# Weight conversion moved from GpSimd to the vector engine, and a part of q's rotation the other way

## The chip, the cores and the metric

One Trainium2 chip, one of its cores. The time is that of one execution on the device, in microseconds (us). The engines are named as the profile names them: PE (matrix multiplies) with PEld (its loads of stationary operands), DVE (vector engine), ACT (scalar engine), POOL (GpSimd), SP (the queue that issues the DMAs).

## What is computed

Rotary attention followed by two feed-forward layers, all in float32 from inputs of which the weights are float64:

```python
q, k, v: (4, 8, 576, 64)
rotate(x) = concat([x1 * cos - x2 * sin, x1 * sin + x2 * cos])      # x1, x2: halves of the last axis
attn = softmax(rotate(q) @ rotate(k).T / 8)                          # per batch and head
x  = (attn @ v) as (2304, 512)
h  = x @ w_in                                                        # (512, 2048)
g  = where(h >= 1, h, where(h <= -1, 0, (h + 1) ** 2 / 4));  x = g @ w_out
h2 = x @ w_in2;  g2 = s * relu(h2) ** 2 + b;                 out = g2 @ w_out2
```

## The kernel before

The heads are taken two at a time: 16 pairs, each with 9 units of queries. For a unit PE makes the scores `sc` (two buffers in PSUM), DVE takes their maximum (`nm`, line 342), ACT the exponential (`p`, line 347), PE turns `p` over and multiplies by v. Every product is made with split operands: a high part of few bits and a low part, so that three products of high and low stand for one of full precision.

A feed-forward layer has 16 slices of weights, each converted in two halves of 128 x 512 (64 conversions in all: 32 per layer). Half of the first layer's slices work beside the attention ("fill" work: `h` and `y` products of the tokens whose attention is done); from about 450 us on only the feed-forward layers are left, and PE runs through `hps` and `yps`.

**Conversion of half a slice** (`convert`, lines 115 to 134). A weight arrives as 8 bytes (`wraw`, two buffers, loaded by SP). ACT scales the upper four bytes into `wa` (line 127). DVE shifts them (128), sets the sign (129) into `wm`, keeps the exponent alone in `wa` (130), and multiplies it by 16 lower bits of the weight (131). ACT rounds `wm` to the high part `hi` (132). POOL takes `wm - hi` and adds `wa`: the low part `lo`. Each of these two POOL operations is cut in two pieces of 256 columns (`pool_tt`, line 91), so one conversion issues 4 POOL instructions. `wa` and `wm` have one buffer each: the next conversion's line 127 waits until POOL has read `wa` of this one. The result goes to the slice's tile `w`, or for 8 halves of the attention's time back into `wraw`, to be parked in DRAM.

**Rotation of the next pair** (`rope_pair`, lines 273 to 283). For each pair `i + 1` while pair `i` runs: POOL multiplies q by the table (line 279, 4 pieces of 288), DVE adds the two products (line 281), ACT writes the high part `qs` (294) and DVE the low part (295). The same for k is all POOL's, and ACT's for its high part (306).

Each engine works its instructions off in order. The order of the instructions in the attention's time is set by a planner from estimated times, with some instructions held behind others (`issue_after`); from line 708 on PE's order is the written one. `do_load` (line 530 on) places the conversions and the rotations: one conversion each two to six units, the rotation of q at unit 0 of each pair.

Of the kernel before, what the change touches and what calls it, by code (L numbers as in the profile page):

```python
# [11 lines left out]
U32 = mybir.dt.uint32  # L12
U16 = mybir.dt.uint16
AF = mybir.ActivationFunctionType
ALU = mybir.AluOpType
# [48 lines left out]
def kernel(ctx, tc, qq, kk, vv, tab, ww1, ww2, s, b, out):  # L64
    nc = tc.nc
# [14 lines left out]
    def pool_tt(out, in0, in1, op, dim=-1):  # L80

        n = out.shape[dim]
        free = 1
        for x in out.shape[1:]:
            free *= x
        k = min(n, -(-free // PW))
        for i in range(k):
            c = [slice(None)] * len(out.shape)
            c[dim] = slice(n * i // k, n * (i + 1) // k)
            c = tuple(c)  # L90
            nc.gpsimd.tensor_tensor(out=out[c], in0=in0[c], in1=in1[c], op=op)  # L91
# [3 lines left out]
    def split(dst_hi, dst_lo, src, hi_eng, lo_eng):  # L95
        if hi_eng is nc.scalar:
            made.append(nc.scalar.copy(dst_hi, src).ins)  # L97
        else:
            hi_eng.tensor_copy(dst_hi, src)
        tt = pool_tt if lo_eng is nc.gpsimd else nc.vector.tensor_tensor  # L100
        tt(out=dst_lo, in0=src, in1=dst_hi, op=ALU.subtract)  # L101
# [7 lines left out]
    class Slice:  # L109
# [5 lines left out]
        def convert(self, raw, pools, hi, lo):  # L115
            if not wide:
                split(hi, lo, raw, nc.scalar, nc.gpsimd)
                return


            top = raw.bitcast(F32).rearrange("p (n t) -> p n t", t=2)[:, :, 1]
            low = raw.bitcast(U16).rearrange("p (n t) -> p n t", t=4)[:, :, 1]
            pool = pools[self.f * 2 + self.made & 1 if len(pools) > 1 else 0]
            a = pool.tile([P, HW], F32, tag="wa", name="wa", bufs=WB)
            m = pool.tile([P, HW], F32, tag="wm", name="wm", bufs=WB)
            au, mu = a.bitcast(U32), m.bitcast(U32)
            nc.scalar.activation(a, top, AF.Copy, scale=2.0 ** -112)
            nc.vector.tensor_scalar(out=mu, in0=au, scalar1=3, scalar2=None, op0=ALU.logical_shift_left)
            nc.vector.scalar_tensor_tensor(out=mu, in0=au, scalar=0x80000000, in1=mu, op0=ALU.bitwise_and, op1=ALU.bitwise_or)  # L129
            nc.vector.tensor_scalar(out=au, in0=mu, scalar1=0xFF800000, scalar2=None, op0=ALU.bitwise_and)  # L130
            nc.vector.scalar_tensor_tensor(out=a, in0=low, scalar=2.0 ** -36, in1=a, op0=ALU.mult, op1=ALU.mult)
            nc.scalar.copy(hi, m)  # L132
            pool_tt(out=m, in0=m, in1=hi, op=ALU.subtract)
            pool_tt(out=lo, in0=m, in1=a, op=ALU.add)

        def load(self, stage, k):
            raw = stage.tile([P, HW], self.ww.dtype, tag="wraw", name="wraw", bufs=RB)
# [107 lines left out]
    def load_qk(i, nm, pieces=WHOLE):  # L245
        bb, hp = divmod(i, NP)
        t = att2.tile([P, 2, S], F32, tag="qkin", name=f"{nm}in", bufs=QB)
        for c in pieces:
            nc.sync.dma_start(out=t[:, :, c], in_=(qq if nm == "q" else kk)[bb, hp, :, :, c])
        qk_in[nm, i] = t  # L250

    def load_v(i):
        bb, hp = divmod(i, NP)
        t = att2.tile([P, 5, 2, D], F32, tag="vin", name="vin", bufs=VB)
        for out, src in ((t[:, :, 1], vv[bb, hp, :, :, 1]), (t[:D, :4, 0], vv[bb, hp, D:, :4, 0]), (t[D:, :4, 0], vv[bb, hp, :D, 1:, 0]), (t[D:, 4, 0], vv[bb, hp, :D, 0, 0])):
            nc.sync.dma_start(out=out, in_=src)
        v_in[i] = t
# [15 lines left out]
    def rope_pair(i, nm, mul, add, lo_eng, pieces=WHOLE):  # L273

        t = qk_in.pop((nm, i))
        tt = {nc.gpsimd: pool_tt, nc.vector: nc.vector.tensor_tensor}
        last = None
        for c in pieces:
            tt[mul](out=t[:, :, c], in0=t[:, :, c], in1=tab_sb[:, :, c], op=ALU.mult)
            r = t[:, 1, c]  # L280
            tt[add](out=r, in0=t[:, 0, c], in1=r, op=ALU.add)
            last = (lay_q if nm == "q" else lay_k)(i, t, c, lo_eng)
        return last
# [3 lines left out]
    def lay_q(i, t, c, lo_eng, heads=range(2)):  # L287

        st = stacks["q", i] = qs_t[i % 2]
        r = t[:, 1, c]  # L290
        for j in heads:
            own, other = SELF[j], SELF[1 - j]
            at = slice(j * QW + c.start, j * QW + c.stop)
            h = nc.scalar.activation(st[own, at], r[own], AF.Copy, scale=0.125)
            m = nc.vector.scalar_tensor_tensor(out=st[other, at], in0=r[own], scalar=0.125, in1=st[own, at], op0=ALU.mult, op1=ALU.subtract)  # L295
        return h.ins, m.ins
# [180 lines left out]
    def turned_by(t, c):  # L477
        nc.vector.tensor_tensor(out=t[:, :, c], in0=t[:, :, c], in1=tab_sb[:, :, c], op=ALU.mult)
        nc.vector.tensor_tensor(out=t[:, 1, c], in0=t[:, 0, c], in1=t[:, 1, c], op=ALU.add)
# [7 lines left out]
    hi, rest = lay_q(0, tq, QP[0], None, [0])  # L487
    with tc.issue_after(hi):
        first = lay_k(0, tk, HALVES[1], [nc.gpsimd, nc.gpsimd], [1])
    hi, rest = lay_q(0, tq, QP[0], None, [1])  # L490
# [39 lines left out]
    def do_load(n):  # L530
        if n < 2:
            with tc.issue_after(maxs[0] if n else rest):
                turned_by(tq, QP[n + 1])
                lay_q(0, tq, QP[n + 1], None)
        if n < len(units):
            i, k = units[n]
            if i + 1 < NPAIR:
                if k == (i == 0):
                    with ExitStack() if i else tc.issue_after(maxs[1]):
                        rope_pair(i + 1, "q", nc.gpsimd if i else nc.vector, nc.vector, None)  # L540
                elif k == 2:
                    with ExitStack() if i else tc.issue_after(exps[2]):
                        rope_pair(i + 1, "k", nc.gpsimd, nc.gpsimd, [nc.gpsimd, nc.vector])
                elif k == 3:
                    load_v(i + 1)
                elif k in (4, 6) and i + 2 < NPAIR:
                    load_qk(i + 2, "q" if k == 4 else "k")

        if n in range(33, 51, 2) or n in range(70, 110, 4):
            with tc.issue_after(exps[n - 14]):  # L550
                convert()

        if n in PARK_AT and parking:
            with tc.issue_after(exps[n - 4]):
                parking.pop(0).park(wst, scratch)
# [31 lines left out]
    def do_fill(n):  # L587
        if n < 48:
            return
        with tc.issue_after(exps[min(n, len(units)) - 4]):  # L590
            run_fill(0.62 if n < 76 else 0.92)

    acts = {"q": do_qk, "l": do_load, "t": do_t, "a": do_av, "f": do_fill}
    for n in range(len(units) + LA):
        with ExitStack() as st:
# [24 lines left out]
    def stage(src, chunks, dst, parts, slices, act, ahead, per):  # L620
# [33 lines left out]
        for i in range(len(steps) + GL):  # L654
# [39 lines left out]
            if i < len(steps):  # L694
                owed += per
                while owed >= 1:
                    with tc.issue_after(mark):
                        convert()
                    owed -= 1

    def cut(n0, n1, n):

        k = -(-(n1 - n0) // n)
        at = [n0 + (n1 - n0) // 16 * i // k * 16 for i in range(k + 1)]
        return [(a, b - a) for a, b in zip(at, at[1:])]
# [5 lines left out]
    a, b, c, d = cut(last, NT, N2A), cut(0, last, N2), cut(last, NT, N2), cut(0, NT, N2)  # L711
# [57 lines left out]
```

## Time and profile before

| | before |
|---|---|
| median of 3 runs | 1138.54 us (1137.49 to 1143.67) |
| profiled execution | 1140.24 us, span 1138.4 us |
| busy: PE, DVE, ACT, POOL | 1091.7, 600.3, 696.9, 536.2 us |
| mean granted PE clock | 0.995 |

The span runs from the first instruction's start to the last one's end. A busy time says how long an engine had an instruction, not whether it worked at its peak. "Idle before" names what ended an engine's wait.

### The profile page before, as it was taken

What the parts mean: (1) busy time and instruction counts of PE and PEld (TensorE: products, weight loads), DVE (VectorE), ACT (ScalarE), POOL (GpSimd) and SP (SyncE); (2) the same over time, 40 slices, a digit from 0 to 9 for tenths busy, and PEclk for the clock granted to TensorE, in tenths of its full rate; (3) what the DMA queues carried; (4) which work ended last, traced back from release to release, by engine and by line L of the source; (5) the groups of instructions that cost most, each with busy time, mean ns of one, the idle gap of its engine ahead of it and who ended that gap; (6) DMA issues with size and microseconds to landing.
All of it is one profiled execution on the core that took longest, in us unless ns stands there. A gap on an engine that the chain in (4) does not pass through costs nothing.

```text
span 1138.4 us, 18638 instructions
## 1 busy us (share of the span) xinstructions
PE 1091.7 (96%) x6720; PEld 981.3 (86%) x6720; DVE 600.3 (53%) x1003; ACT 696.9 (61%) x1472; POOL 536.2 (47%) x716
## 2 busy tenths in 40 slices
PE   3999999889999999999999999999999999999998
PEld 3666677778898989999999999998888889888887
DVE  6889898887676753454656555343333242221121
ACT  4777777766776775565555444476766756555543
POOL 7979887885572322355656624343443452011000
PEclk9999899999999999999999999999999999999999
DMA  7565755544564433455344434313322331220210
GB/s 223 166 183 168 190 149 177 175 134 155 165 180 148 134 110 89 157 161 166 109 145 139 147 100 120 100 55 104 105 70 90 104 110 54 90 81 29 67 51 34
DMA packets 89756, 140.46 MB, mean 123 GB/s; under 512 B 28864, under 2 KB 66752, under 8 KB 89664
## 3 DMA queue, kind: packets, MB, share of 16 engines
q1 hardware_dynamic: 89664, 139.27, 40.2%
q8 instruction: 53, 0.87, 0.3%
q14 instruction: 39, 0.32, 0.1%
HBM read 95.22 MB, written 30.74 MB: 111 GB/s over the span
## 4 chain that ended last, share of the span: by engine, by line
PE 78%; DVE 7%; DMA 4%; ACT 4%; POOL 4%; issue 2%; SPq 1%; POOLq 0%; ACTq 0%; DVEq 0%
PE hps L171 30%; PE yps L682 10%; PE yps L684 10%; PE yps L683 10%; PE sc L340 5%; PE h L171 3%; PE av L388 3%; PE tp L362 3%; PE y L171 2%; POOL kin L91 2%; DVE nm L342 2%; ACT p L347 2%; DMA kin<-in_k 1%; DVE qs L295 1%; DVE wm L129 1%
## 5 line engine op out<-in xcount | busy, mean ns | idle before, releaser
L171 PE MATMUL hps<-xh,w 128*128 128x464 f32 (+5 forms) x1216 | 344.5, 348 | 0.0
L171 PEld LDWEIGHTS hps<-xh,w 128*128 128x128 f32 x1216 | 221.8, 188 | 14.8
L682 PE MATMUL yps<-gh,w 128*128 128x464 f32 (+5 forms) x608 | 211.7, 348 | 0.5 <-ACT ys L465 0.5
L684 PE MATMUL yps<-gh,w 128*128 128x464 f32 (+5 forms) x608 | 211.6, 348 | 0.0
L171 PE MATMUL hps<-xl,w 128*128 128x464 f32 (+5 forms) x608 | 211.5, 348 | 0.0
L683 PE MATMUL yps<-gl,w 128*128 128x464 f32 (+5 forms) x608 | 211.4, 348 | 0.0
L91 POOL TENSOR_TENSOR xl<-xs,xh 128x232 fp32r<-128x232 f32 (+5 forms) x172 | 125.5, 758 | 171.2 <-ACT xh L97 170.9
L91 POOL TENSOR_TENSOR wm<-wm,w 128x256 f32<-128x256 f32 x112 | 100.3, 916 | 208.0 <-ACT w L132 167.1
L101 DVE TENSOR_TENSOR gl<-ar,gh 128x464 fp32r<-128x464 f32 (+1 forms) x80 | 59.0, 737 | 263.5 <-ACT gh L97 263.5
L340 PE MATMUL sc<-kh,qs 128*128 128x288 f32 x336 | 103.7, 330 | 32.6 <-ACT p L347 20.6
L342 DVE TENSOR_REDUCE nm<-sc 128x1 f32<-128x576 f32 x144 | 107.7, 752 | 39.7 <-PE sc L340 38.9
L347 ACT ACTIVATE p<-sc,nm 128x576 f32<-128x576 f32 x144 | 106.7, 743 | 32.6 <-DVE nm L342 32.0
L682 PEld LDWEIGHTS yps<-gh,w 128*128 128x128 f32 x608 | 114.1, 188 | 8.1 <-ACT ys L465 0.8
L683 PEld LDWEIGHTS yps<-gl,w 128*128 128x128 f32 x608 | 114.1, 188 | 7.5
L684 PEld LDWEIGHTS yps<-gh,w 128*128 128x128 f32 x608 | 114.1, 188 | 7.4
L171 PEld LDWEIGHTS hps<-xl,w 128*128 128x128 f32 x608 | 114.1, 188 | 7.3
L202 ACT ACTIVATE ar<-hps 128x464 f32<-128x464 f32 (+1 forms) x80 | 44.4, 555 | 121.7 <-PE hps L171 121.2
L340 PEld LDWEIGHTS sc<-kh,qs 128*128 128x128 f32 x336 | 65.1, 196 | 50.7 <-ACT p L347 28.8
L362 PE MATMUL tp<-ident,p 128*128 128x128 f32 x576 | 90.3, 281 | 5.5 <-ACT p L347 3.3
L340 PE MATMUL sc<-kz,qs 128*128 128x288 f32 x336 | 95.2, 303 | 0.0
L101 DVE TENSOR_TENSOR gl<-ac,gh 128x288 fp32r<-128x288 f32 (+3 forms) x112 | 72.6, 650 | 40.6 <-ACT gh L97 40.0
L91 POOL TENSOR_TENSOR w<-wm,wa 128x256 fp32r<-128x256 f32 x112 | 87.9, 803 | 0.2
(87 smaller groups left out, 1981.9 us busy)
## 6 DMA issues: line engine op xcount, KB each, us to landing
wraw<-in_ww SPq DMA_DIRECT2D x64, 512.0 KB, 3.8
kin<-in_k SPq DMA_DIRECT2D x15, 576.0 KB, 4.9
qin<-in_q SPq DMA_DIRECT2D x15, 576.0 KB, 3.9
kh<-kin SPq DMA_DIRECT2D x60, 144.0 KB, 2.6
xs<-y1d SPq DMA_DIRECT2D x32, 232.0 KB, 2.5
xs<-xd SPq DMA_DIRECT2D x44, 144.0 KB, 2.4
yd<-ys SPq DMA_DIRECT2D x40, 144.0 KB, 2.6
xd<-u SPq DMA_DIRECT2D x16, 288.0 KB, 2.4
```

The lines of the kernel that those rows point to most:

```text
L91: nc.gpsimd.tensor_tensor(out=out[c], in0=in0[c], in1=in1[c], op=op)
L101: tt(out=dst_lo, in0=src, in1=dst_hi, op=ALU.subtract)
L171: m = nc.tensor.matmul(out_ps, l, r, start=(i == 0), stop=(i == n - 1))
L202: nc.scalar.activation(r, h, AF.Relu)
L340: nc.tensor.matmul(sc[:, half, o:o + n], l, r[:, k0:k0 + n], start=m == 0, stop=m == len(todo) - 1)
L342: maxs[i * 9 + k] = nc.vector.tensor_reduce(out=nm, in_=sc[:, :, :288], axis=AX.XY, op=ALU.max, negate=True).ins
L347: exps[i * 9 + k] = nc.scalar.activation(p, sc[:, :, :288], AF.Exp, bias=nm, scale=1.0, accum_out=sums_t[i][:, col:col + 1]).ins
L362: m = nc.tensor.transpose(v[:, c, :], p[:, c * P:(c + 1) * P], ident)
L388: nc.tensor.matmul(ps[j * D:(j + 1) * D, :n], v[:, kt, j, :], pt[g][:, kt, j, :], start=kt == 0, stop=False)
L682: nc.tensor.matmul(acc, wh, gh, start=f == 0, stop=False)
L683: nc.tensor.matmul(acc, wh, gl, start=False, stop=False)
L684: nc.tensor.matmul(acc, wl, gh, start=False, stop=last)
```

## The change

Two edits. In `convert` the shifted bits are masked at once, so that `wm` is the high part before ACT copies it; the bits below the mask are taken from `wraw` as whole numbers, joined with the 16 lower ones, and scaled by the exponent into the low part. DVE now makes six instructions for a conversion instead of four, POOL none instead of four. The fifth of the six overwrites `wm`, which ACT's copy reads. In `do_load` the addition of q's two products for pairs 4 to 11 goes from DVE to POOL, where it is cut into two pieces of 288 columns.

```diff
-            nc.vector.tensor_scalar(out=mu, in0=au, scalar1=3, scalar2=None, op0=ALU.logical_shift_left)
+            nc.vector.tensor_scalar(out=mu, in0=au, scalar1=3, scalar2=0x7FFFF000, op0=ALU.logical_shift_left, op1=ALU.bitwise_and)
             nc.vector.scalar_tensor_tensor(out=mu, in0=au, scalar=0x80000000, in1=mu, op0=ALU.bitwise_and, op1=ALU.bitwise_or)
-            nc.vector.tensor_scalar(out=au, in0=mu, scalar1=0xFF800000, scalar2=None, op0=ALU.bitwise_and)
-            nc.vector.scalar_tensor_tensor(out=a, in0=low, scalar=2.0 ** -36, in1=a, op0=ALU.mult, op1=ALU.mult)
+            nc.vector.tensor_scalar(out=au, in0=raw.bitcast(U32).rearrange("p (n t) -> p n t", t=2)[:, :, 1], scalar1=0x1FF, scalar2=None, op0=ALU.bitwise_and)
+            nc.vector.scalar_tensor_tensor(out=a, in0=au, scalar=65536.0, in1=low, op0=ALU.mult, op1=ALU.add)
             nc.scalar.copy(hi, m)
-            pool_tt(out=m, in0=m, in1=hi, op=ALU.subtract)
-            pool_tt(out=lo, in0=m, in1=a, op=ALU.add)
+            nc.vector.tensor_scalar(out=mu, in0=mu, scalar1=0xFF800000, scalar2=None, op0=ALU.bitwise_and)
+            nc.vector.scalar_tensor_tensor(out=lo, in0=a, scalar=2.0 ** -36, in1=m, op0=ALU.mult, op1=ALU.mult)
...
-                        rope_pair(i + 1, "q", nc.gpsimd if i else nc.vector, nc.vector, None)
+                        rope_pair(i + 1, "q", nc.gpsimd if i else nc.vector, nc.gpsimd if 3 <= i < 11 else nc.vector, None)
```

## Rows read from the trace of the kernel before

**Rows 1.** Windows by stage: length, busy time (instructions), granted clock, DMA share, GB/s.

```profile
core 0: us, PE busy (x) PEld busy (x) DVE busy (x) ACT busy (x) POOL busy (x), PEclk, DMA share, GB/s
50.00:300.00 250.00, 228.79 (x1692) 185.84 (x1691) 207.22 (x343) 177.88 (x425) 194.00 (x251) 0.98 0.57 168
300.00:450.00 150.00, 147.57 (x1160) 132.31 (x1155) 91.28 (x173) 100.65 (x257) 54.42 (x80) 1.00 0.43 132
450.00:950.00 500.00, 499.47 (x2809) 474.25 (x2808) 228.75 (x377) 295.93 (x575) 229.70 (x303) 1.00 0.37 117
```

**Rows 2.** Windows for line 127 alone: it runs once for each conversion.

```profile
50.00:300.00 250.00, 12.28 (x18) 0.98 0.57 168
300.00:450.00 150.00, 4.03 (x6) 1.00 0.43 132
450.00:950.00 500.00, 26.84 (x40) 1.00 0.37 117
```

**Rows 3.** PE's timeline: start, length, instruction, [PE idle before it, releaser].

```profile
129.63 0.40 PE L340 MATMUL sc<-kh,qs 128*128 128x288 f32 x1 [1.84 <-ACT p L347]
...
189.11 0.40 PE L340 MATMUL sc<-kh,qs 128*128 128x288 f32 x1 [2.48 <-ACT p L347]
...
218.92 0.40 PE L340 MATMUL sc<-kh,qs 128*128 128x288 f32 x1 [2.97 <-ACT p L347]
...
242.34 0.40 PE L340 MATMUL sc<-kh,qs 128*128 128x288 f32 x1 [1.48 <-ACT p L347]
```

**Rows 4.** Chain of waits before the PE stall at 189 us: start, length, what.

```profile
183.81 0.70 POOL w L91
...
184.54 0.68 ACT wa L127
...
186.34 0.85 DVE wm L129
```

**Rows 5.** DVE's timeline around the PE stalls at 130 and 219 us.

```profile
126.45 1.27 DVE L281 TENSOR_TENSOR qin<-qin 128x576 f32<-128x576 f32 x1 [1.31 <-POOL qin L91]
...
215.67 0.62 DVE L128 TENSOR_SCALAR wm<-wa 128x512 uint32<-128x512 uint32 x1 [1.65 <-ACT wa L127]
```

**Rows 6.** Windows behind two of these stalls: PE's granted clock.

```profile
130.00:138.00 8.00, 7.23 (x37) 5.74 (x37) 5.53 (x9) 6.00 (x14) 6.84 (x11) 0.57 0.40 92
...
218.00:224.00 6.00, 5.08 (x26) 4.11 (x28) 5.20 (x9) 5.31 (x13) 4.89 (x6) 0.72 0.61 163
```

**Rows 7.** Lines by form, DVE, 50 to 300 us: count, busy us, mean ns, idle before.

```profile
L131 DVE SCALAR_TENSOR_TENSOR wa<-wraw,wa 128x512 f32<-128x512 uint16 x18 | 16.5, 916 | 0.3
L129 DVE SCALAR_TENSOR_TENSOR wm<-wa,wm 128x512 uint32<-128x512 uint32 x18 | 16.3, 904 | 0.3
...
L281 DVE TENSOR_TENSOR qin<-qin 128x576 f32<-128x576 f32 x11 | 12.5, 1134 | 6.6 <-POOL qin L91 6.6
L128 DVE TENSOR_SCALAR wm<-wa 128x512 uint32<-128x512 uint32 x18 | 11.0, 612 | 3.9 <-ACT wa L127 3.6
L130 DVE TENSOR_SCALAR wa<-wm 128x512 uint32<-128x512 uint32 x18 | 10.5, 584 | 0.2
```

**Rows 8.** Lines by form, POOL, 50 to 300 us.

```profile
L91 POOL TENSOR_TENSOR wm<-wm,w 128x256 f32<-128x256 f32 x32 | 28.2, 901 | 7.5 <-DVE wa L130 4.4 <-ACT w L132 2.0 <-ACT r L421 1.2
L91 POOL TENSOR_TENSOR w<-wm,wa 128x256 fp32r<-128x256 f32 x32 | 25.7, 818 | 0.2
L91 POOL TENSOR_TENSOR kin<-kin 128x288 f32<-128x288 f32 x21 | 18.8, 903 | 0.2
...
L91 POOL TENSOR_TENSOR wraw<-wm,wa 128x256 fp32r<-128x256 f32 x4 | 3.2, 792 | 0.0
L91 POOL TENSOR_TENSOR wm<-wm,wraw 128x256 f32<-128x256 f32 x4 | 3.1, 789 | 1.9 <-ACT wraw L132 1.9
```

**Rows 9.** Tile `wa`: count, ns of one (min/median/max), first and last start.

```profile
L129 DVE SCALAR_TENSOR_TENSOR wm<-wa,wm x64: 655/693/1304, 62.1 to 939.0; 128x512 uint32<-128x512 uint32 x64
L130 DVE TENSOR_SCALAR wa<-wm x64: 396/427/1027, 64.7 to 939.8; 128x512 uint32<-128x512 uint32 x64
L131 DVE SCALAR_TENSOR_TENSOR wa<-wraw,wa x64: 676/693/1282, 67.7 to 940.2; 128x512 f32<-128x512 uint16 x64
```

## The prediction

> **What bounds the kernel now.** First the windows by stage [rows 1]. From 450 us to 950 us PE has an instruction for 499.47 of 500 us: nothing done to DVE or POOL can shorten that, only lengthen it. From 300 to 450 us PE lacks 2.4 us. From 50 to 300 us it lacks 250 - 228.79 = 21.2 us, and there DVE is busy for 207.22 us (83%) and POOL for 194.00 us (78%). The first 50 us come before the first conversion, and the stretch behind 950 us after the last. So what the change can win is in these 21.2 us and in the time PE ran at a lower clock there. PE's timeline shows the four largest stalls of that stage [rows 3]: 1.84, 2.48, 2.97 and 1.48 us, 8.8 us together, each ended by an exponential of ACT. The other 12.4 us are many small ones. The chain of waits behind the stall at 189 us [rows 4] reads backwards from it: ACT's copy of a conversion's high part stood in front of the exponential; that copy waited for DVE's line 129, this for ACT's line 127, and line 127 started at the moment when POOL had finished with the single buffer `wa` of the conversion before. At 219 us DVE itself stood idle for 1.65 us for that line 127 [rows 5] with the maximum of the scores queued behind. At 130 us DVE waited 1.31 us for POOL's product of q and then took 1.27 us for the sum [rows 5], and the maximum behind it came late. The fourth, at 242 us, I count like the second without going further into it. Then the clock: in the 8 us behind the first stall PE was granted 0.57 and in the 6 us around the third 0.72 [rows 6], where full is 2.4 GHz and the lower level 1.2 GHz: 8 x 0.43 + 6 x 0.28 = 5.1 us of full-speed work lost, behind idle PE both times. What the edits can touch is therefore 8.8 + 5.1 = 13.9 us.
>
> **POOL, removed and added.** 18 of the 64 conversions lie in 50 to 300 us, 6 in 300 to 450, 40 behind [rows 2]. In the first stage POOL loses 28.2 + 25.7 + 3.2 + 3.1 = 60.2 us [rows 8]. It gains the sums of q for 8 pairs, two pieces each; the same form with the same shape is k's sum at 903 ns [rows 8]: 16 x 0.903 = 14.4 us. POOL goes from 194.0 to 148.2 us (59%), a quarter less.
>
> **DVE, added and removed.** The mask put into line 128 is a second operation of an instruction that runs anyway; I take its 612 ns [rows 7] as unchanged, since line 129 of the same width also makes two operations and what sets it apart is its second tensor. The mask of the exponent moves from fourth to fifth place at the same price. The multiplication of line 131 becomes a multiplication and an addition on two tensors, as before 916 ns. New are the low bits from `wraw` and the last product. The last product is line 131's or 129's form: 916 ns in this stage, 676 ns when nothing disturbs it [rows 7, 9]. For the low bits no row shows a one-tensor mask whose source steps over every other word: the dense one takes 584 ns in this stage and 396 ns at least [rows 7, 9], and line 131, which also reads `wraw` in steps, 916 ns. I take 584, the row of the same operation; less than 396 is excluded because no 512-column instruction of these lines is shorter. So 18 x (0.584 + 0.916) = 27.0 us are added, between 19.3 and 33.0. Pairs 4 to 11 lose line 281: 8 x 1.134 = 9.1 us [rows 7].
>
> VectorE: DVE Perf Modes of the Trainium skill (section What auto-detection actually checks) says that an instruction with a single source goes at two elements per cycle if source and destination lie in SBUF with fitting outer dimensions, and names no condition on the step for that mode. No run here shows it for a stepped source; by the page the stepped mask would cost what the dense one does, which leaves the sum as it is, and by the row of line 131 it would cost 18 x 0.332 = 6.0 us of DVE more.
>
> DVE's instructions also get longer when POOL is busy: in this stage lines 129, 130 and 131 average 904, 584 and 916 ns against medians of 693, 427 and 693 [rows 7, 9], 18 x (0.211 + 0.157 + 0.223) = 10.6 us. A quarter less POOL gives back a quarter, 2.5 us (bounds: 0 and, for all of it, 10.6). Net DVE gets 27.0 - 9.1 - 2.5 = 15.4 us more: 222.6 us, 89%. With the ends of the two new instructions it is 7.7 to 21.4 us.
>
> **What of this reaches PE.** (a) Stalls that go. At 130 us the wait and the sum in front of the maximum go (2.58 us against a stall of 1.84): all of it. At 219 us DVE's idle 1.65 us goes; the two long instructions of the conversion that follow remain. At 189 us, and so at 242, POOL's hold on `wa` goes but the conversion's own DVE and ACT work stays: half, 1.98 us. That is 5.5 of 8.8 us; the same share of the clock's 5.1 us is 3.2. Together -8.7 us, between 0 (something else is late just then) and -13.9.
> (b) The busier DVE. The 12.4 us of small stalls are the price of a DVE at 83%. If what waits in front of an engine grows as busy time over idle time, 207.2/42.8 = 4.84 becomes 222.6/27.4 = 8.12, and the small stalls grow by 0.68 x 12.4 = 8.4 us. Two score buffers cover part: I take half, +4.2 us, between 0 and, with the upper DVE load (10.7 for 8.12) and the full price, +15.0. Less than 0 is excluded by a load that is larger at both ends.
> (c) The new wait. The fifth instruction overwrites `wm` and must wait for ACT's copy; behind it on DVE stand the next maximum and the copies out of PSUM, for which ACT's exponential and PE wait. Between the two instructions the low bits and their sum take 0.58 + 0.92 = 1.5 us, while the copy itself starts when line 129 is done; so the wait shows only where ACT has much in front. The nearest row is DVE's wait for ACT at the start of a conversion, 3.6 us over 18 [rows 7]; a good quarter at PE, +1.0 us, between 0 and 3.6.
> (d) q's sum on POOL ends later: 2 x 0.903 = 1.81 us against 1.13, 0.67 us more for 8 pairs. ACT's split of q waits for it, with exponentials behind. It belongs to the next pair, so a whole pair of 9 units hides it: 0, and 5.4 us if ACT reaches it at once each time.
> (e) Later stages: between 300 and 450 us 6 conversions with DVE at 91 of 150 us: 0. From 450 to 950 us 40 x 1.5 = 60 us come to DVE's 228.75 of 500 [rows 1, 2]. PE hides them, working three steps behind the splits that DVE makes: 0. If that cover went, PE would wait for each conversion's last instruction, up to 40 x 0.92 us; nothing in PE's 499.47 us speaks for it.
>
> Sum: -8.7 + 4.2 + 1.0 = -3.5 us. Against the profiled execution's 1140.24 us (span 1138.4 and 1.84 around it) that is 1136.7; it lies 1.7 us above the median of the three runs, from which the forecast is 1138.54 - 3.5 = **1135.0 us**.
>
> **Rivals.** *The vector engine becomes the bound, slower.* In 50 to 300 us the maximum of the scores queues behind six conversion instructions instead of four. For it: DVE is already the busiest of the helpers. Against: PE's stall rows point to POOL at the largest places. Price: the full +15.0, 3.6 for the copy, less 8.7: +9.9, 1148.4 us. It decides from the DVE share at which the full price eats the credit: 12.4 x (r/4.84 - 1) = 7.7, r = 7.85, which is 88.7% of the stage, just about what I forecast; so only the half taken for the score buffers stands between the two.
> *The stalls come back elsewhere, no change.* `wa` and `wm` still have one buffer, now released by DVE's last instruction, and the planner's order shifts; the credit halves: -4.35 + 5.2 = +0.9, 1139.4 us. For it: the small stalls, which POOL does not cause.
> *POOL was the whole matter, clearly faster.* All 13.9 us come back with the clock, DVE's load at its lower end costs half its price (215/35 is 6.12, 0.26 x 12.4 / 2 = 1.6): -12.3, 1126.2 us. For it: both clock dips lie behind such stalls. Against: line 129, which stays, takes up to 1.304 us [rows 9] on its own.
>
> **How the numbers follow.** Forecast 0.44 (its own range 1130 to 1140), DVE the bound 0.18, no change 0.16, POOL the whole matter 0.22. No change within 0.5% is 1132.85 to 1144.2 us, about what a measurement can tell here. Faster: 0.16 of the forecast's 0.44 and 0.21 of the last, 0.37. Slower: 0.16 of the second and 0.01, 0.17. The rest, 0.46, is the same. The range 1125 to 1147 leaves out some 0.06 below (the better half of the last rival is near its edge) and 0.10 above.
>
> **What would show it.** PE's idle time in 50 to 300 us falls from 21.2 to about 18 us and its clock there rises above 0.98; POOL is busy near 150 us and DVE near 222 us; the stepped mask near 0.58 us; no row where ACT's line 127 starts as POOL ends; DVE's wait for the copy under 4 us. Wrong: stalls at PE behind DVE's fifth instruction, a DVE above 90%, ACT waiting for POOL's q, or a PE that falls short after 450 us.

## The result and the profile after

The change makes the kernel slower: a median of 1148.95 us over 7 runs (1144.63 to 1152.05) against 1140.40 us over 7 runs of before. The ratio is 1.0073 [1.0053, 1.0093], which is +8.3 us [6.0, 10.6]; forecast were -3.5 us.

| | before | after |
|---|---|---|
| median of the runs | 1140.40 us | 1148.95 us |
| profiled execution, its span | 1140.24, 1138.4 us | 1144.63, 1142.9 us |
| busy: PE, DVE, ACT, POOL | 1091.7, 600.3, 696.9, 536.2 us | 1092.2, 639.9, 696.5, 353.2 us |
| PE idle in the span | 46.7 us | 50.7 us |
| mean granted clock, mean over the runs | 0.9945 (before's runs in the experiments; 0.995 in the profiled one) | 0.992 |

The profiled execution of after is its fastest; it shows only 4.5 us of span more, 4.0 of it PE's idle time. So its rows are read for where the time goes, and the sizes are taken from the ratios over all runs. One execution of after_hold and one of before_dve2 below took some 1796 us at a granted clock of 0.56; the ratios leave them out.

Windows by stage of after, in the columns of [rows 1]:

```profile
50.00:300.00 250.00, 227.21 (x1673) 184.85 (x1674) 211.78 (x365) 173.57 (x419) 156.05 (x195) 0.99 0.58 169
300.00:450.00 150.00, 145.97 (x1143) 129.35 (x1142) 97.10 (x185) 99.70 (x253) 32.75 (x52) 1.00 0.42 126
450.00:950.00 500.00, 499.26 (x2818) 474.13 (x2817) 257.87 (x459) 297.18 (x579) 105.24 (x146) 1.00 0.38 117
```

PE lacks 22.8 us in the first stage (21.2 before) and 4.0 in the second (2.4 before); behind 450 us it is as full as it was. POOL fell by 38 us in the first stage, and PE got nothing for it. The same stage in three parts, first of before, then of after:

```profile
50.00:130.00 80.00, 72.45 (x522) 50.88 (x520) 69.34 (x116) 59.12 (x138) 64.45 (x85) 1.00 0.64 183
130.00:210.00 80.00, 74.50 (x553) 63.35 (x552) 68.52 (x114) 57.49 (x138) 65.37 (x84) 0.96 0.53 156
210.00:300.00 90.00, 81.84 (x621) 71.61 (x621) 69.37 (x114) 61.27 (x150) 64.18 (x84) 0.98 0.56 166
```

```profile
50.00:130.00 80.00, 72.41 (x517) 50.72 (x517) 76.62 (x131) 58.73 (x136) 61.25 (x74) 1.00 0.66 189
130.00:210.00 80.00, 70.97 (x525) 59.76 (x526) 71.07 (x125) 57.09 (x138) 45.76 (x58) 0.98 0.53 156
210.00:300.00 90.00, 83.83 (x632) 74.37 (x631) 64.10 (x113) 57.76 (x145) 49.04 (x65) 0.98 0.56 163
```

The stage average hides the shape: in the first 80 us DVE is busy 96% of the time (87% before), with 8 of the 18 conversions there instead of 5 (windows for line 127). PE has lost nothing in those 80 us (72.41 us for 72.45). Between 130 and 210 us it loses 3.5 us against before, and it wins 2.0 back behind.

PE's timeline of after, which answers to [rows 3]:

```profile
131.62 0.40 PE L340 MATMUL sc<-kh,qs 128*128 128x288 f32 x1 [1.92 <-ACT p L347]
...
191.64 0.40 PE L340 MATMUL sc<-kh,qs 128*128 128x288 f32 x1 [2.27 <-ACT p L347]
...
221.12 0.44 PE L375 MATMUL tr<-ident,p 128*128 128x128 f32 x2 [1.72 <-ACT ys L465]
...
223.24 0.49 PE L340 MATMUL sc<-kh,qs 128*128 128x288 f32 x1 [1.57 <-ACT p L347]
```

Stalls at about 130, 190 and 220 us are still there, though no row has ACT's line 127 start as POOL ends; the one at 242 us is gone, and two more, at 98 and 148 us (2.08 and 1.52 us), are not among before's four. The clock is at full behind 130 us, where before had 0.57. It dips behind 191 us, where before had 1.00 (190 to 198 us), and behind 221 us, where before had dipped too (0.79 in the same window):

```profile
130.00:138.00 8.00, 5.20 (x37) 4.06 (x39) 7.97 (x13) 6.47 (x15) 7.86 (x11) 1.00 0.55 166
190.00:198.00 8.00, 6.36 (x36) 5.73 (x38) 6.24 (x13) 7.27 (x17) 0.00 (x0) 0.79 0.14 31
218.00:226.00 8.00, 4.72 (x27) 4.23 (x26) 4.98 (x8) 5.32 (x13) 5.61 (x9) 0.84 0.66 194
```

What is late at 191 us in place of POOL's hold on `wa`? The chain of waits of after that ends there (start, length, what):

```profile
176.23 2.19 POOL qin L91 x2
178.42 4.12 POOL kin L91 x4
182.54 0.77 POOL qin L91
183.31 1.54 POOL kin L91 x2
184.85 0.02 issue
184.88 0.67 ACT kin L306
185.55 0.49 ACT pt L367
186.04 0.74 ACT p L347 x2
...
190.86 0.74 ACT p L347 x2
191.60 0.04 issue
191.64 0.40 PE sc L340
```

Line 306 is ACT's copy of k's high part, here for pair 10, whose first exponential comes at 260.2 us. It is needed some 75 us later, yet it stands in ACT's queue in front of exponentials that PE wants now, and ACT waited 1.97 us at it for POOL's rotation of k. That rotation stands behind q's, and q's behind the load of q. The copy for pair 10 in before, then in after:

```profile
183.16 0.67 ACT L306 CAST kin<-kin 128x576 fp32r<-128x576 f32 x1 [0.63 <-POOL kin L91]
```

```profile
184.88 0.67 ACT L306 CAST kin<-kin 128x576 fp32r<-128x576 f32 x1 [1.97 <-POOL kin L91]
```

ACT came to it at 182.5 us in before and at 182.9 us in after, so ACT was not early. What was later is POOL's rotation, by 1.7 us: the load of q was issued at 169.55 us where before issued it at 167.49, and q's sum now stands on POOL too. ACT's waits for line 306 in 50 to 300 us, before and after (waited for: us in total, times, longest):

```profile
ACT kin L306 <- POOL kin L91: 2.9, 4, 0.8
```

```profile
ACT kin L306 <- POOL kin L91: 7.8, 6, 2.0
ACT kin L306 <- DMA xs<-xd: 3.2, 1, 3.2
```

And POOL's row of q in after, from the lines by form, as [rows 8]: it now waits 25.2 us for q's load, where it waited 11.5 us before:

```profile
L91 POOL TENSOR_TENSOR qin<-qin,tab_sb 128x288 f32<-128x288 f32 x40 | 35.7, 921 | 28.5 <-DMA qin<-in_q 25.2 <-DVE wm L133 3.4
```

DVE's lines by form in after, which answer to [rows 7]:

```profile
L131 DVE SCALAR_TENSOR_TENSOR wa<-wa,wraw 128x512 f32<-128x512 uint32 x18 | 16.3, 905 | 0.2
L129 DVE SCALAR_TENSOR_TENSOR wm<-wa,wm 128x512 uint32<-128x512 uint32 x18 | 16.3, 903 | 0.1
L134 DVE SCALAR_TENSOR_TENSOR w<-wa,wm 128x512 fp32r<-128x512 f32 x16 | 13.2, 822 | 0.1
L130 DVE TENSOR_SCALAR wa<-wraw 128x512 uint32<-128x512 uint32 x18 | 11.2, 624 | 0.3
L133 DVE TENSOR_SCALAR wm<-wm 128x512 uint32<-128x512 uint32 x18 | 11.2, 620 | 0.0
L128 DVE TENSOR_SCALAR wm<-wa 128x512 uint32<-128x512 uint32 x18 | 9.8, 543 | 3.0 <-ACT wa L127 2.9
```

The two new instructions are 130 (the stepped mask) and one of 131 and 134. The durations of 130 and 131 are as forecast, and 134 is shorter (822 and, into `wraw`, 686 ns for 916).

### The profile page after: what moved, and what is told of

It is laid out like the page before. It is cut to its first block, busy times and chain, and to the rows that moved or that the text cites. A ratio compares the mean times of both kernels' runs of the same rounds, so it can differ in the third digit from the quotient of the medians.

```text
span 1142.9 us, 18413 instructions
## 1 busy us (share of the span) xinstructions
PE 1092.2 (96%) x6720; PEld 980.8 (86%) x6720; DVE 639.9 (56%) x1123; ACT 696.5 (61%) x1472; POOL 353.2 (31%) x476
## 4 chain that ended last, share of the span: by engine, by line
PE 76%; DVE 7%; DMA 6%; ACT 4%; POOL 4%; issue 2%; SPq 1%; POOLq 0%; ACTq 0%; DVEq 0%
PE hps L171 30%; PE yps L682 10%; PE yps L683 10%; PE yps L684 10%; PE sc L340 4%; PE h L171 4%; PE av L388 3%; PE y L171 2%; PE tp L362 2%; POOL kin L91 2%; DVE nm L342 2%; ACT p L347 2%; DMA qin<-in_q 1%; DMA xs<-xd 1%; POOL qin L91 1%
## 5 line engine op out<-in xcount | busy, mean ns | idle before, releaser
L91 POOL TENSOR_TENSOR xl<-xs,xh 128x232 fp32r<-128x232 f32 (+5 forms) x172 | 128.2, 773 | 482.0 <-ACT xh L97 475.6
L101 DVE TENSOR_TENSOR gl<-ar,gh 128x464 fp32r<-128x464 f32 (+1 forms) x80 | 53.1, 664 | 255.5 <-ACT gh L97 255.5
L97 ACT CAST gh<-ac 128x288 fp32r<-128x288 f32 (+3 forms) x112 | 52.3, 467 | 50.3 <-DVE ac L194 49.7
L101 DVE TENSOR_TENSOR gl<-ac,gh 128x288 fp32r<-128x288 f32 (+3 forms) x112 | 61.8, 552 | 36.6 <-ACT gh L97 36.0
L194 DVE SCALAR_TENSOR_TENSOR ac<-hps,ac 128x288 f32<-128x288 f32 (+3 forms) x72 | 37.6, 522 | 74.0 <-ACT ac L193 73.6
```

## The experiments

Three theories stood for the loss: the two added DVE instructions of each conversion (DVE the bound; V in what was expected); q's sum on POOL (Q); and the order that the planner makes anew (P), in which a copy for a later pair holds up ACT (C). Each run is compared with runs of before on the same chip.

**One half at a time.** conv_only is after with q's sum back on DVE; q_only is before with q's sum on POOL.

```diff
# conv_only, against after
-rope_pair(i + 1, "q", ..., nc.gpsimd if 3 <= i < 11 else nc.vector, None)
+rope_pair(i + 1, "q", ..., nc.vector, None)
# q_only, against before: the same line the other way
```

> The new conversion alone, q's sums all on the vector engine as before. Theory (the vector engine becomes the bound while conversions run beside the attention): 9 us of vector work more than the changed kernel has in 50 to 300 us, so at least as slow as it, 1149 to 1153 us. Rival Q (the sum of q on GpSimd is what costs): back to 1138 to 1142. Rival P (any edit makes the planner order PE's queue anew, and the order decides): anything between 1136 and 1152, and no more stalls behind the vector engine than in the changed kernel.

Measured: 1151.44 us, 1.0092 [1.0076, 1.0108].

> The old conversion, and q's sum for pairs 4 to 11 on GpSimd. Theory: the vector engine loses 9 us before 210 us, GpSimd gains 14 us; 1136 to 1142 us, no slower than before. Rival Q: 1146 to 1150. Rival P: anything between 1136 and 1152.

Measured: 1148.01 us, 1.0061 [1.0044, 1.0077], in the range of rival Q, as conv_only was in that of the theory. Each half alone loses, and together they lose no more than one of them: the halves don't add. In q_only POOL has the old conversion and 12.3 us of sums besides, and hands over the weights late, for 6.8 us of PE's time in the stage. PE's timeline of q_only:

```profile
156.47 0.40 PE L171 MATMUL y<-gh,w 128*128 128x288 f32 x1 [1.69 <-POOL w L91]
...
183.12 1.53 PE L171 MATMUL y<-gh,w 128*128 128x288 f32 x4 [5.12 <-POOL w L91]
```

That is not all of it: ACT waits at k's copy as long as in after, 5.6 us of it just before the longer of these stalls. No run gave q_only the hold that is tried below, so its loss isn't divided between the two.

```profile
ACT kin L306 <- POOL kin L91: 8.2, 3, 5.6
```

With the new conversion POOL has room: after against conv_only is 1.0073 against 1.0092, and the intervals overlap. So q's sum on POOL is no cause of after's loss.

**Is the loss in the attention's time?** late_only uses the new conversion only for the weights converted behind the attention.

```diff
+            if len(scratch) == 1:
+                ...  # the conversion of before
+            else:
+                ...  # the conversion of after
```

> The old conversion beside the attention, the new one for the conversions after it, q's sums as before. Theory: after the attention PE hides the vector engine's work, 1139 to 1142 us, as before, with PE busy for over 499 of the 500 us behind 450 us. A rival by which the wait for ACT's copy or the six instructions cost wherever they stand: 40 of the 64 conversions are here, 1143 to 1147.

Measured: 1139.28 us, 0.9982 [0.9967, 0.9997]; PE has 499.26 of the 500 us behind 450 us. The new conversion costs nothing there; the loss is made while the attention runs.

**The two added instructions.** no_low_bits is after without lines 130 and 131: the lower bits of the weights are left out of the low part.

```diff
-            nc.vector.tensor_scalar(out=au, in0=raw..., scalar1=0x1FF, scalar2=None, op0=ALU.bitwise_and)
-            nc.vector.scalar_tensor_tensor(out=a, in0=au, scalar=65536.0, in1=low, op0=ALU.mult, op1=ALU.add)
```

> The changed kernel without the two instructions that read the lower bits (the low part is then built from another operand of the same shape, so the weights' lower bits are left out): four vector instructions for a conversion as before, none on GpSimd. Theory: the vector engine has 1.5 us less for each conversion, and GpSimd's relief is all that remains: 1134 to 1140 us. Rival P: as slow as the changed kernel or unrelated to it, 1136 to 1152. If GpSimd's relief is worth nothing: 1140.

Measured: 1140.39 us, 1.0001 [0.9985, 1.0017]. Without them the loss is gone: 0.0072 x 1140 = 8.2 us. But nothing is gained either, though DVE is down to 195.8 us in the first stage and POOL to 151.0. So something else ate the credit, and ACT's wait in no_low_bits says what it may be: the wait for POOL's k is longer still (line 304 there is 306 of after, with two lines gone above it).

```profile
ACT kin L304 <- POOL kin L91: 13.1, 7, 3.5
```

before_dve2 puts the same two instructions as dead work into before, ahead of the shift.

```diff
+            nc.vector.tensor_scalar(out=mu, in0=raw..., scalar1=0x1FF, scalar2=None, op0=ALU.bitwise_and)
+            nc.vector.scalar_tensor_tensor(out=m, in0=mu, scalar=65536.0, in1=low, op0=ALU.mult, op1=ALU.add)
             nc.vector.tensor_scalar(out=mu, in0=au, scalar1=3, scalar2=None, op0=ALU.logical_shift_left)
```

> The kernel before with the two added vector instructions (low bits read in steps, and a joining of the same form) made into wm ahead of each conversion's shift, their result not used; GpSimd as before. Theory V: 27 us of vector time in 50 to 300 us at 0.27 us each, 1146 to 1150, about as the changed kernel. If the loss came from the planner's order or from the wait for ACT's copy instead: 1140 to 1143.

Measured: 1168.07 us, 1.0224 [1.0201, 1.0248], far above what was expected. It is no clean price: the dead work writes `wm`, so DVE waits for POOL at the head of 6 of 17 conversions, which before it did not. The line by form of that instruction, and the window behind 450 us, where PE now lacks 6 us:

```profile
L128 DVE TENSOR_SCALAR wm<-wraw 128x512 uint32<-128x512 uint32 x17 | 12.2, 717 | 9.4 <-POOL w L91 9.3
```

```profile
450.00:950.00 500.00, 493.84 (x2814) 467.50 (x2815) 262.50 (x443) 281.34 (x557) 224.02 (x288) 1.00 0.37 113
```

**The copy that stands too early.** after_hold holds k's rotation, with its copy, behind the exponential nine units earlier; before_hold does the same to before. (In after only the first pair's is held.)

```diff
-                    with ExitStack() if i else tc.issue_after(exps[2]):
+                    with tc.issue_after(exps[max(2, n - 9)]):
                         rope_pair(i + 1, "k", nc.gpsimd, nc.gpsimd, [nc.gpsimd, nc.vector])
```

> The changed kernel with ACT's copy of k's high part held behind the exponential one pair earlier (it stands two pairs and more ahead of its use and waits on GpSimd for up to 3.2 us there). Theory C (GpSimd's relief is lost because that copy now waits for k's rotation, which waits for q's load): the copy's waits go and with them the stalls at 191 and 223 us, 1142 to 1146 us. Theory V alone (only the two added vector instructions per conversion cost): 1147 to 1151.

Measured: 1141.64 us, 1.0007 [0.9994, 1.002].

> The kernel before with the same hold. Theory C: the copy waits only 2.9 us there in 50 to 300 us, so little to win, 1137 to 1141. If the hold is worth something for another reason, it gains as much here as in the changed kernel.

Measured: 1141.51 us, 1.0011 [0.9995, 1.0027]. One line takes 0.0066 x 1140 = 7.5 us out of after and nothing out of before. Pair 10's copy now starts at 206.1 us in place of 184.9, the rows of ACT waiting at line 306 are gone, and POOL still waits for q's load as long as it did (27.9 us):

```profile
POOL qin L91 <- DMA qin<-in_q: 27.9, 8, 4.8
```

So POOL's own wait costs nothing here; what went together with the 7.5 us are ACT's waits at the copy. That PE's stalls went with them the rows do not show. PE's largest wait in 50 to 300 us, in after and in after_hold:

```profile
PE sc L340 <- ACT p L347: 18.1, 18, 2.3
```

```profile
PE sc L340 <- ACT p L347: 19.2, 18, 2.7
```

The stalls at 131 and 191 us are shorter in after_hold and others have come; ACT waits 29.5 us for the maximum where it waited 22.6. Over the whole span PE is idle for 49.3 us in after_hold's profiled execution and for 50.7 in after's.

before_null shifts the hold of before's conversions by one unit, to see what a mere other order does.

```diff
-            with tc.issue_after(exps[n - 14]):
+            with tc.issue_after(exps[n - 13]):
                 convert()
```

> The kernel before with the conversions' hold moved by one unit: the same work, PE's order the same, a few instructions of the other engines in another order. How much an order alone moves the time: theory V 1138.5 to 1142; if the planner's order decides, a change of 4 us or more either way.

Measured: 1141.13 us, 0.9999 [0.9984, 1.0014]. This small change of the order moves nothing; none was tried on after.

**The credit by itself.** no_low_hold is no_low_bits with the hold (lower bits left out again); conv_hold is conv_only with the hold.

```diff
# no_low_hold, against after: both edits
-            ...  # lines 130 and 131
-                    with ExitStack() if i else tc.issue_after(exps[2]):
+                    with tc.issue_after(exps[max(2, n - 9)]):
```

> The changed kernel with the hold of ACT's copy, and without the two instructions that read the lower bits (left out as in the run without the hold): both suspected costs taken away. Theory (two costs that add up: ACT's copy waiting for GpSimd, and two vector instructions per conversion): 1131 to 1136 us, clearly below the kernel before. If the vector instructions cost nothing once the copy is held: 1140 to 1142, as the held kernel. If the copy only matters where the vector engine is full: 1138 to 1141, as without the hold.

Measured: 1136.04 us, 0.9954 [0.9938, 0.9971].

> The new conversion alone with the hold, q's sums all on the vector engine. Theory: 9 us more vector work before 210 us than in the held kernel, at a quarter to a third of a us each, 1143.5 to 1146 us. If q's sum on GpSimd is neutral: 1141 to 1142.

Measured: 1140.71 us, 1.0006 [0.9993, 1.0019]. The hold is worth 0.0086 x 1140 = 9.8 us in conv_only, 7.5 in after, 5.4 in no_low_bits, nothing in before. In 50 to 300 us ACT waited at the copy for POOL's k for 8.1, 7.8 (and 3.2 for a transfer), 13.1 and 2.9 us in these four. So where ACT waits much the hold pays and where it hardly waits it does not, but the gain doesn't follow the size of the wait. Windows of no_low_hold, then of after_hold:

```profile
50.00:130.00 80.00, 71.92 (x518) 50.30 (x517) 76.47 (x123) 62.67 (x142) 58.70 (x74) 1.00 0.72 203
50.00:300.00 250.00, 232.25 (x1732) 190.39 (x1731) 200.40 (x339) 180.67 (x431) 151.34 (x199) 0.99 0.61 173
```

```profile
50.00:130.00 80.00, 71.07 (x512) 49.70 (x511) 76.09 (x130) 59.50 (x138) 60.11 (x73) 1.00 0.65 187
50.00:300.00 250.00, 227.52 (x1688) 186.08 (x1687) 213.03 (x370) 176.84 (x425) 158.31 (x198) 0.99 0.58 170
```

Without the two instructions PE is busy 4.7 us longer in the stage than in after_hold, and 3.5 us longer than in before: here the freed POOL shows at PE. (No_low_bits has 231.13 us there, in a profiled execution that is its fastest.)

**Better versions.** hold_paced starts after_hold's conversions later, against the crowd at 50 to 130 us; hold_qall gives POOL q's sum for all pairs from 4 on.

```diff
# hold_paced, against after_hold
-            with tc.issue_after(exps[n - 14]):
+            with tc.issue_after(exps[n - 6]):
# hold_qall, against after_hold
-rope_pair(i + 1, "q", ..., nc.gpsimd if 3 <= i < 11 else nc.vector, None)
+rope_pair(i + 1, "q", ..., nc.gpsimd if i >= 3 else nc.vector, None)
```

> The held kernel with the conversions held 6 instead of 14 units behind, so that fewer of them fall into 50 to 130 us, where the vector engine is busy for 95%. If the pile-up there is what is left of the loss: 1136 to 1140 us. If the vector work costs the same wherever it stands beside the attention: 1141 to 1143. If weights come late: stalls at y products, 1144 or more.

Measured: 1143.26 us, 1.0022 [1.0007, 1.0038]. Starting later does not help, though 6 conversions instead of 8 lie in 50 to 130 us and DVE is busy there for 70.02 of 80 us, as in before: the theory of the pile-up missed.

> The held kernel with q's sum on GpSimd for the pairs 12 to 15 too. Behind 230 us the vector engine loses 4.5 us and its waits for GpSimd's product (8.4 us before 300 us); PE lacks little there: 1139 to 1142 us.

Measured: 1138.50 us, 0.9980 [0.9965, 0.9994], a little under what was expected and the fastest of the kernels that compute everything, together with late_only. It beats after by 0.9% and before by 0.2%.

## Why the prediction was wrong

Between before and after stand two kernels, no_low_hold and after_hold, that cut the loss into terms (each ratio against its own runs of before, times 1140 us):

| step | term | forecast | measured |
|---|---|---|---|
| before to no_low_hold | POOL relieved, stalls that go; (a) with (c) | -8.7 + 1.0 = -7.7 | -5.2 [-7.1, -3.3] |
| to after_hold | the two added instructions; (b) | +4.2 | +6.0, about ±2.4 |
| to after | k's rotation not held | no term | +7.5, about ±2.7 |
| sum | | -3.5 | +8.3 |

The division depends on the order of the steps. Without the hold POOL's relief is worth nothing (no_low_bits, 1.0001) and the two instructions cost 8.2 us; the hold is worth 5.4 us without them and 7.5 with them. So either of the two costs, taken away, gives the whole loss back.

**The step that failed** is the list of what reaches PE: it has no term for the place in the order that the planner gives to the work around the edits. Under (d) the prediction looked at the queue behind POOL's rotation, but only at ACT's split of q, found a whole pair of slack and put 0. The slack was right and beside the point: a copy that has 75 us to spare still stops an engine that works in order, if it stands in the queue before what it waits for is done. The copy's place hardly moved (pair 10's stands after the 67th exponential where it stood after the 68th); what moved is the end of POOL's rotation. POOL, a fifth less busy, came to q before its load had landed, k's rotation waited behind q's and ended later than in before, and ACT waited at the copy. What the runs show is the price of that order, 7.5 us by the hold; that ACT's wait is the way by which it reaches PE is not shown. The rival "The stalls come back elsewhere" named the planner's order, without a place, and priced it at half the credit, 4.35 us; it cost more than the 5.2 us that the relief gave.

**(a)** The waits named were removed: line 127 never starts at POOL's release any more, and stalls at 130, 190 and 220 us came back with other causes. As a size, -5.2 us together with (c) is two thirds of the forecast. No run splits the -5.2: DVE's 6.8 us less in no_low_hold (200.40 against 207.22) is in it too, and so is `wraw`, which nothing behind line 127 reads in that kernel and which is free for the next load sooner. POOL came to 156.05 us for 148.2, since its other pieces got longer: q's products, for one, from 853 to 921 ns.

**(b)** Was about right, +6.0 for +4.2. By rows the instructions came out as forecast: 18 x (0.624 + 0.905) = 27.5 us for 27.0, or 25.1 us as the difference of all the rows of a conversion. The 2.5 us that a less busy POOL was to give back did not come in lines 129 and 131, which stayed at 0.90 us. DVE's busy time in the stage did not come out as forecast: 211.8 for 222.6 us. Part of this is relief in a line I had not counted (line 101 fell from 761 to 528 ns, 4.4 us), part is that less was done in the stage (87 maxima for 88, 16 of line 101 for 17). The crowding between 50 and 130 us is not what cost: PE lost nothing there in after, no_low_hold has it too (76.47 of 80 us) and is the fastest of all, and hold_paced, without it, is no faster than after_hold. By which waits the two instructions, and the later release of `wraw` that comes with them, cost 6 us stays open. So the prediction's queue formula over the stage average gave about the right size by a path that the rows do not bear out, which is luck in part.

The rival *The vector engine becomes the bound* came within a microsecond of the time, 1148.4 us, but with +15.0 us for DVE. The runs give DVE +6.0, and after_hold, with as busy a DVE, is 7.5 us faster than after: its time was right by luck, its mechanism only half.

**(c)** Right: DVE's wait for ACT's copy at the fifth instruction is 1.8 us in the whole run, and 0.6 more at a half that goes back into `wraw`, for bounds of 0 to 3.6:

```profile
DVE wm L133 <- ACT w L132: 1.8, 2, 1.1
```

**(d)** Right by itself: with room on POOL the sum is neutral (after_hold against conv_hold 1.0007 against 1.0006). With the old conversion it goes with 7 us of loss (q_only), so the change's two halves do not add; how much of that is POOL's lack of room and how much k's copy was not separated.

**(e)** Right, by late_only and by the 499.26 us behind 450 us; between 300 and 450 us PE lost 1.6 us, forecast 0.

What stays open: the mean clock over the runs is 0.992 in after and 0.997 in after_hold, 0.9945 in before. How much of the 7.5 us is lost in waiting and how much in the lower clock behind the waits was not separated. An estimate from these clocks: PE's 1092 us of work take 0.005 x 1092 = 5.5 us longer at the lower one, if all of it stretches with the clock, which would be most of the 7.5. The two profiled executions, with 0.996 and 0.997, lie only 2.6 us apart. The hold moves the rotation of k as a whole; no run moved ACT's copy alone, so that ACT's wait is the mechanism is read from the chain and from the rows that went, against PE's rows, which hardly changed; and the price of 7.5 us is that of the hold. Since the gain of the hold is not in the order of ACT's waits, a part of it may be POOL's other work, which the hold lets forward. Or the planner's order in after was an unlucky one that any other change would have bettered: no run tested that on after, though the hold gained in all three kernels with the new conversion. And the stall at 220 us stays in after_hold (2.7 us), with a cause that was not followed up.

## What to carry to other kernels

When an edit frees an engine whose order a planner writes, look at what the planner will put into the gap, and whether a part of it lands on another engine that works in order. An operation with much time to spare still stops such an engine where what it waits for isn't done; try whether a hold on it pays, as it did here. Price an edit's halves together, since here each loses alone and one line of order decides the rest. Read the busy share in short windows, since a stage average hides a crowd (96% of 80 us behind an 85% stage); and read in the same window whether PE lost anything, since here it did not.

## What the runs showed of the hardware

The mask whose source steps over every other word took 624 ns in the stage, the dense one of line 133 took 620; over the whole run the step costs nothing either (min/median/max in ns):

```profile
L130 DVE TENSOR_SCALAR wa<-wraw x64: 386/427/949, 62.1 to 940.5; 128x512 uint32<-128x512 uint32 x64
```

```profile
L133 DVE TENSOR_SCALAR wm<-wm x64: 410/421/1112, 63.5 to 941.6; 128x512 uint32<-128x512 uint32 x64
```

VectorE: DVE Perf Modes of the Trainium skill (section What auto-detection actually checks), which for a single source at two elements per cycle names no condition on the step, agrees with these rows. The shift with the mask as second operation took 543 ns where the shift alone had taken 612 [rows 7], and 427 for 428 ns in the median of the run: the second operation on the same data came free. DVE's line 101, which the change does not touch, fell by 30% in the stage, where POOL was busy for 156 us instead of 194, while lines 129 and 131 kept their 0.90 us; no run shows that POOL is the reason.
